# Last output tile in two column halves with a bank and a store each, and q transposes of loop rounds 3 to 5 one place later behind the row transposes

## The chip, the core and the metric

The kernel runs on one core of a Trainium2 chip. The metric is the device time of one execution in microseconds (us); less is better. Before the change the median of four runs is 278.32 us (277.8 to 278.83).

The core has a matrix engine (TensorE, PE in the profile; its weight loads are the row PEld), a vector engine (VectorE, DVE), a scalar engine (ScalarE, ACT), GpSimd (POOL) and SyncE (SP). Each runs its own instructions in order. SP, ACT and POOL can issue DMAs; their issuing sides are SPq, ACTq and POOLq in the profile. Sixteen DMA engines carry all transfers. Matrix products are accumulated in PSUM, which has eight banks.

## What is computed

Attention without softmax, RMS-normalised for each head, and then a two-layer network with a PReLU:

```python
kv  = einsum('bhsd,bhse->bhde', k, v)            # 8 batches, 8 heads, 576 rows, 64 columns
out = einsum('bhsd,bhde->bhse', q, kv)
x   = out / sqrt(mean(out*out, -1) + 1e-6) * g_norm   # reshaped to 4608 tokens x 512
h   = x @ w_in                                   # 512 -> 2048
g   = maximum(h, 0) + alpha * minimum(h, 0)
y   = g @ w_out                                  # 2048 -> 512, float32
```

## The kernel before

**Blocks and rounds.** The 4608 tokens are worked in nine blocks of 512 (`W`, `NW`). After a head part for block 0, a loop `for w in range(1, NW)` (L929) runs rounds of 16 units `u` each. A unit of round `w` issues one group of the first layer for block `w` (`m1_group`, L488: four matmuls of 512 columns at L472, one ACT instruction at L479 and one DVE instruction at L483), seven matmuls of the second layer for block `w - 1` (`prod_mm`, L608, matmul at L631), and the part of the attention for block `w + 1` that a table assigns to that unit (`attention`, L906). All engine orders are written out by hand (a manual schedule): instructions run on each engine in the order in which the code issues them.

**The second layer as seven products.** Tokens, hidden units and output columns are each cut in two, and the product is put together from seven half-size products instead of eight. Each product has 16 matmuls of 256 columns: `i` counts them, `a, c = divmod(i, 8)`, `a` is the group of 128 tokens and `c` the step of the sum. Their order is `Y_ORDER = (1, 6, 2, 7, 5, 4, 3)` (L685). Products 1 and 2 go to PSUM bank X (pool `ps_y`), 6, 7 and 4 to Y (bank `h0`), 5 and 3 to Z (pool `ps_q`). `y_read` (L656) reads partial sums from the banks: the four output quarters are c11, c22, c21 and c12. In the last round (`w == NW - 1`) bank Z is split by `a` (`y_bank`, L592): `yZ0` stays in `ps_q`, `yZ1` takes bank `h2`, which the first layer no longer uses.

**The tail.** After the loop only products are left, for block 8 (L972 to L989). The last 16 matmuls are product 3: eight for `a = 0`, then `y_read(w, "c12", (0,))` adds `yZ0` to a stored partial sum (`u2`) on DVE (L678) and stores 128 rows by 256 columns; then eight for `a = 1`, and the last line, L989, does the same with `yZ1`. That last tile is rows 4224 to 4351, columns 256 to 511, of the output. Product 5 uses the same two Z banks and is read by `y_read(w, "c22")`. The stores take their queue in turn from `store_engines` (`put`, L505; the DMA's line is L508). Output tiles in SBUF come from one pool of four buffers (`ysb_p`, L63), used in rotation.

**Transposes on SP.** From block 4 on (`W_ROW = 3`) the attention output is computed by rows: for each of four row tiles `i` of a block, `rows_mm` (L405, matmuls at L414, L420 and L424), `rows_ssq`, `rows_rs` and `rows_norm` (L449: a DVE instruction at L452 that writes `x_rows`, and then a transposing DMA on SP at L457 that writes 128 columns of `xt`, the input of the next block's first layer). In units 5, 7, 9 and 11 (`norm` in `ATT_ROW`, L894) the row tiles 0 to 3 are normalised and their transposes issued. The q of a later batch is transposed by the same queue: `dma_t` (L333) issues up to five transposing DMAs (L338), one for 128 rows of q each, the fifth for the 64 that remain. When it does so is said by a table:

```python
QT_AT = {False: {7: (0, 1), 9: (2,), 11: (3, 4)}, True: {8: (0,), 10: (1,), 12: (2, 3, 4)}}
...
if w + 1 < B:
    dma_t(w + 1, QT_AT[w == W_ROW].get(u, ()))
```

`attention(w + 1, u)` is called in round `w`, so the `False` row serves the loop rounds 3, 4 and 5, which transpose q of batches 5, 6 and 7. The `True` row serves round 2. In units 7, 9 and 11 a q transpose stands on SP behind the row transpose of the same unit and ahead of the row transpose of the next. GpSimd loads the k, q and v of a later batch at the start of each round (`load_gated`, L186); its first load writes the buffer that the fifth q transpose of the round before has read.

Of the kernel before, what the change touches and what calls it, by code (L numbers as in the profile page):

```python
# [9 lines left out]
FP32 = mybir.dt.float32  # L10
# [7 lines left out]
def kernel(  # L18
# [11 lines left out]
    nc = tc.nc  # L30
# [5 lines left out]
    P = 128  # L36
    NPAIR = H // 2
    W = 512
    NW = N_TOK // W
# [23 lines left out]
    ysb_p = ctx.enter_context(tc.tile_pool(name="ysb", bufs=4))  # L63
    ps_h = ctx.enter_context(tc.tile_pool(name="psh", bufs=1, space=bass.MemoryType.PSUM))
# [12 lines left out]
    def early_pair(eng, nm, tag):  # L77
# [14 lines left out]
            name=nc.get_next_instruction_name(),  # L92
# [25 lines left out]
    for r in range(P // D):  # L118
        nc.sync.dma_start(
            out=alpha_row[NF : NF + 1, r * D : (r + 1) * D], in_=g_norm[:].unsqueeze(0)  # L120
# [7 lines left out]
    for i in range(NBUF):  # L128
        t = {}
        for nm in ("k", "v", "q") if i < 2 else ("k", "v"):  # L130
            n = 1 if nm == "v" else T0 if i == 0 else NT
# [201 lines left out]
    def dma_t(b, ts=tuple(range(NT))):  # L333
        qt = qt_sb[b % 2][:, :, PAD : PAD + S]
        for t in ts:
            c0, c1 = t * P, min((t + 1) * P, S)
            src = stages[b, "q"][:, t] if t < TPP else buf_of(b, "q")[0:REM, TPP]
            nc.sync.dma_start_transpose(  # L338
                out=qt[:, :, c0:c1], in_=src.rearrange("p h d -> p (h d)"),
            )  # L340
        for j in range(NPAIR):
            qts[b, j] = qt_sb[b % 2][:, j, PAD : PAD + S]
# [159 lines left out]
    store_engines = [(nc.gpsimd,)]  # L502
    store_turn = [0]

    def put(dst, src):  # L505
        engs = store_engines[0]
        store_turn[0] += 1
        engs[store_turn[0] % len(engs)].dma_start(out=dst, in_=src)  # L508

    def row_pieces(n0):  # L510
        i = 0
        while i < P:
            b, r = divmod(n0 + i, S)
            np_, nt = (P0, T0) if b == 0 else (P, TPP)
            if b < B_NAT and r < np_ * nt:
                t, p = divmod(r, np_)
                cnt = min(P - i, np_ - p)
                yield i, cnt, b, t, p
            else:
                cnt = P - i if b >= B_NAT else min(P - i, S - r)  # L520
                yield i, cnt, None, n0 + i, 0
            i += cnt

    def grid(b):
        np_, nt = (P0, T0) if b == 0 else (P, TPP)
        return out[b * S : b * S + np_ * nt, :].rearrange("(p t) m -> p t m", t=nt)

    def store_rows(n0, src, c0, c1):
        for i, cnt, b, t, p in row_pieces(n0):
            dst = out[t : t + cnt, c0:c1] if b is None else grid(b)[p : p + cnt, t, c0:c1]  # L530
            put(dst, src[i : i + cnt])
# [7 lines left out]
    HC = D_MODEL // 2  # L539
    NK = NF // 2  # L540
# [48 lines left out]
    ybank = {}  # L589
    part = {}  # L590

    def y_bank(w, n, a):  # L592
        pool, tag = {"X": (ps_y, "y"), "Y": (ps_h, "h0"), "Z": (ps_q, "q")}[n]
        if w == NW - 1 and n == "Z":
            key = (w, n, a)
            if a == 1:
                pool, tag = ps_h, "h2"
            if key not in ybank:
                t = pool.tile([P, HC], FP32, name=f"yZ{a}", tag=tag)
                ybank[key] = t  # L600
                return t[:], True
            return ybank[key][:], False
        fresh = (w, n) not in ybank
        if fresh:
            ybank[w, n] = pool.tile([P, 2, HC], FP32, name=f"y{n}", tag=tag)
        return ybank[w, n][:, a, :], fresh

    def prod_mm(w, n, i):  # L608
        a, c = divmod(i, NK)
        bank, fresh = y_bank(w, {1: "X", 2: "X", 6: "Y", 7: "Y", 4: "Y", 5: "Z", 3: "Z"}[n], a)  # L610
        cols = slice(a * P, (a + 1) * P)
        hi_cols = slice(HW + a * P, HW + (a + 1) * P)
        k, r = divmod(c, 2)
        if n == 1:
            lhs = gts[w, k][:, r, cols]
        elif n == 2:
            lhs = gts[w, k + KQ][:, r, cols]
        elif n == 4:
            lhs = gts[w, k + KQ][:, r, hi_cols]
        else:  # L620
            lhs = sums[w, {6: 2, 7: 3, 5: 1, 3: 4}[n], k][:, r, cols]
        q, rr = divmod(c, GW)
        if n == 1:
            rhs = w_out_sb[q][:, rr, 0:HC]
        elif n == 2:
            rhs = w_out_sb[q + WQ // 2][:, rr, 0:HC]
        elif n == 3:
            rhs = w_out_sb[q + WQ // 2][:, rr, HC:D_MODEL]
        else:
            rhs = wsum[{4: 4, 5: 1, 6: 2, 7: 3}[n]][:, c, :]  # L630
        nc.tensor.matmul(  # L631
            out=bank, lhsT=lhs, rhs=rhs, start=fresh, stop=(c == NK - 1), skip_group_check=True,
        )

    def quad_out(w, r, h, src, subs=(0, 1)):
        n0 = w * W + r * HW
        if n0 >= B_NAT * S and len(subs) == 2:
            put(
                out[n0 : n0 + HW, h * HC : (h + 1) * HC].rearrange("(a p) m -> p a m", p=P),
                src[:],  # L640
            )
            return
        one, two = list(row_pieces(n0)), list(row_pieces(n0 + P))
        if len(subs) == 2 and all(
            x[2] is not None and (*x[:3], x[3] + 1, x[4]) == y for x, y in zip(one, two)
        ):
            for i, cnt, b, t, p in one:
                put(
                    grid(b)[p : p + cnt, t : t + 2, h * HC : (h + 1) * HC],
                    src[i : i + cnt],  # L650
                )
            return
        for a in subs:
            store_rows(n0 + a * P, src[:, a, :], h * HC, (h + 1) * HC)

    def y_read(w, what, subs=(0, 1)):  # L656
        if what == "p1":
            part[w, 1] = u_p.tile([P, 2, HC], FP32, name="p1")
            nc.scalar.copy(out=part[w, 1][:], in_=ybank[w, "X"][:])
            return  # L660
        if what in ("u2", "u3"):
            part[w, what] = u_p.tile([P, 2, HC], FP32, name=what)
            nc.vector.tensor_add(
                out=part[w, what][:], in0=ybank[w, "Y"][:], in1=part[w, 1][:]
            )
            return
        y_sb = ysb_p.tile([P, 2, HC], FP32, name="y_sb")
        if what == "c11":
            nc.scalar.copy(out=y_sb[:], in_=ybank[w, "X"][:])
        else:  # L670
            other = part[w, {"c21": 1, "c22": "u3", "c12": "u2"}[what]]
            if what == "c21":
                nc.vector.tensor_add(out=y_sb[:], in0=ybank[w, "Y"][:], in1=other[:])  # L673
            elif w < NW - 1:
                nc.vector.tensor_add(out=y_sb[:], in0=ybank[w, "Z"][:], in1=other[:])
            else:
                for a in subs:
                    nc.vector.tensor_add(  # L678
                        out=y_sb[:, a, :], in0=ybank[w, "Z", a][:], in1=other[:, a, :]
                    )  # L680
        if w < NW - 1:
            store_engines[0] = (nc.sync if what == "c12" else nc.gpsimd,)
        quad_out(w, int(what[1]) - 1, int(what[2]) - 1, y_sb, subs)

    Y_ORDER = (1, 6, 2, 7, 5, 4, 3)  # L685
    Y_LIST = [(n, i) for n in Y_ORDER for i in range(2 * NK)]
    PER = len(Y_LIST) // NF
# [21 lines left out]
    def h_at(i):  # L709
# [7 lines left out]
        out=alpha_ps[:], lhsT=alpha_row[0 : NF + 1, 0:P], rhs=ident[0 : NF + 1, 0 : NF + 1],  # L717
# [6 lines left out]
        out=beta_sb[:], in0=alpha_ps[:, 0:NF], scalar1=-1.0, scalar2=1.0, op0=ALU.mult, op1=ALU.add,  # L724
# [176 lines left out]
                at_row.setdefault(at if what == "kv" else at + d, []).append((what, j))  # L901
        ATT_ROW[first] = at_row
    ROWS = {"kv": row_kv, "mm": rows_mm, "ssq": rows_ssq, "rs": rows_rs, "norm": rows_norm}
    QT_AT = {False: {7: (0, 1), 9: (2,), 11: (3, 4)}, True: {8: (0,), 10: (1,), 12: (2, 3, 4)}}

    def attention(w, u):  # L906
        if W_ROW <= w < NW:
# [3 lines left out]
            if w + 1 < B:  # L911
                dma_t(w + 1, QT_AT[w == W_ROW].get(u, ()))
        elif w < NW:
# [15 lines left out]
    for w in range(1, NW):  # L929
        if w + 2 < B:  # L930
            load_gated(w + 2)
        for u in range(NF):
            if w >= W_ROW - 1 and u in R_FIRST:
                y_read(w - 1, R_FIRST[u])
# [12 lines left out]
            if w > 2 and u == 0:  # L947
                y_read(w - 2, "c12")
# [23 lines left out]
    w = NW - 1  # L972
    store_engines[0] = (nc.sync, nc.scalar)
    Y_READS[13] = Y_READS.pop(14)
    for u in range(NF):
        unit_sums(NW, u)
        if u == 0:
            y_read(w - 1, "c12")
        for i in range(u * PER, (u + 1) * PER):
            prod_mm(w, *Y_LIST[i])  # L980
            if i == len(Y_LIST) - NK - 1:
                y_read(w, "c12", (0,))
        for what in Y_READS.get(u, ()):
            if what == "c21":
                store_engines[0] = (nc.scalar, nc.gpsimd, nc.sync, nc.gpsimd)
                store_turn[0] = -1
            y_read(w, what)
            store_engines[0] = (nc.sync, nc.scalar)
    y_read(w, "c12", (1,))  # L989


# [28 lines left out]
```

## Time and profile before

| | |
|---|---|
| median of four runs | 278.32 us (277.8 to 278.83) |
| the profiled execution | 278.83 us |
| its span, first to last instruction | 277.1 us |
| outside the span | 1.73 us (278.83 - 277.1) |
| PE busy | 269.3 us, 97% of the span |
| DVE busy | 231.6 us, 84% |
| ACT busy | 155.7 us, 56% |
| last matmul of the chain ends | 273.57 us |
| last DVE addition | 273.65 us, lasts 0.42 us |
| last store issued (SP) | 274.10 us, 128 KB |

A line of the profile's tables gives the line of the kernel, the engine, the operation, the output and the inputs by their names in the program (numbers of buffers left out), the shape, and the count. A timeline or chain line begins with the start in us from the beginning of the span and the duration in us. A duration of a DMA-issuing instruction is the time that its queue took to issue it; the time to landing is counted from there to the arrival of the data and is shown in the table of DMA issues. Matmuls are pipelined, so the time of one in a stream is the distance between starts, not the duration that its own row shows.

### The profile page before, as it was taken

What the parts mean: (1) busy time and instruction counts of PE and PEld (TensorE: products, weight loads), DVE (VectorE), ACT (ScalarE), POOL (GpSimd) and SP (SyncE); (2) the same over time, 40 slices, a digit from 0 to 9 for tenths busy, and PEclk for the clock granted to TensorE, in tenths of its full rate; (3) what the DMA queues carried; (4) which work ended last, traced back from release to release, by engine and by line L of the source; (5) the groups of instructions that cost most, each with busy time, mean ns of one, the idle gap of its engine ahead of it and who ended that gap; (6) DMA issues with size and microseconds to landing.
All of it is one profiled execution on the core that took longest, in us unless ns stands there. A gap on an engine that the chain in (4) does not pass through costs nothing.

```text
span 277.1 us, 5185 instructions
## 1 busy us (share of the span) xinstructions
PE 269.3 (97%) x1928; PEld 173.3 (63%) x1928; DVE 231.6 (84%) x446; ACT 155.7 (56%) x285; POOL 84.4 (30%) x119
## 2 busy tenths in 40 slices
PE   7899999999999999999999999999999999999994
PEld 2434544555766676667666766676666666666784
DVE  7559739988789979997999889988997999887862
ACT  3567447789989846654565456545545554444210
POOL 8743453670913337229121731100111011000200
PEclk9999999999999999999999999999999999999999
DMA  7999999999996579979985799520322032201223
GB/s 152 193 207 198 198 202 189 208 127 177 139 173 109 126 105 140 176 171 121 182 144 117 111 172 174 126 78 0 78 76 78 0 83 73 76 0 40 74 81 114
DMA packets 86621, 34.53 MB, mean 125 GB/s; under 512 B 58804, under 2 KB 84932, under 8 KB 86596
## 3 DMA queue, kind: packets, MB, share of 16 engines
q0 software_dynamic: 57488, 24.35, 67.1%
q1 hardware_dynamic: 28212, 8.90, 16.3%
q10 hardware_dynamic: 896, 0.95, 1.1%
q8 instruction: 15, 0.25, 0.4%
q14 instruction: 10, 0.08, 0.1%
HBM read 36.71 MB, written 9.44 MB: 167 GB/s over the span
## 4 chain that ended last, share of the span: by engine, by line
PE 79%; DMA 12%; DVE 4%; issue 1%; ACT 1%; POOL 1%; DVEq 0%; ACTq 0%; POOLq 0%
PE h_ps L472 37%; PE yY L631 14%; PE yX L631 10%; PE yZ L631 9%; DMA w_in_sb<-in_moe_w_in_dram 5%; DMA vst<-in_v_dram 5%; PE kv_ps L348 3%; DMA qst<-in_q_dram 2%; PE y L497 2%; PE or_ps L414 2%; DVE gt L483 1%; PE ot_ps L370 1%; DVE x_rows L452 1%; PE ssq_ps L386 1%; DVE xt L395 1%
## 5 line engine op out<-in xcount | busy, mean ns | idle before, releaser
L472 PE MATMUL h_ps<-xt,w_in_sb 128*128 128x512 f16 x576 | 145.2, 379 | 0.4 <-DVE y_sb L673 0.2
L479 ACT ACTIVATE m_sb<-h_ps 128x512 f32<-128x512 f32 x144 | 86.1, 599 | 82.0 <-PE h_ps L472 80.4
L483 DVE SCALAR_TENSOR_TENSOR gt<-m_sb,beta_sb,h_ps 128x512 f16<-128x512 f32 x144 | 106.9, 745 | 24.7 <-ACT m_sb L479 21.7
L472 PEld LDWEIGHTS <-w_in_sb 128*128 128x128 f16 x576 | 54.6, 98 | 42.9 <-issue 1.0
L508 POOL DMA_DIRECT2D out_dram<-y_sb x36 | 23.2, 647 | 140.3 <-ACT rstd_r L444 43.8
L631 PEld LDWEIGHTS <-s 128*128 128x128 f16 x512 | 50.1, 98 | 19.2
L631 PEld LDWEIGHTS <-gt 128*128 128x128 f16 x384 | 37.6, 98 | 14.8
L631 PE MATMUL yY<-wsum,s 128*128 128x256 f16 x256 | 36.3, 273 | 0.0
L631 PE MATMUL yX<-w_out_sb,gt 128*128 128x256 f16 x256 | 35.1, 273 | 0.0
L159 POOL DMA_DIRECT2D qst<-in_q_dram x20 | 17.7, 917 | 2.0 <-DMA vst<-in_v_dram 2.0
L631 PE MATMUL yZ<-w_out_sb,s 128*128 128x256 f16 x128 | 17.6, 273 | 0.0
L631 PE MATMUL yZ<-wsum,s 128*128 128x256 f16 x128 | 17.6, 273 | 0.0
L631 PE MATMUL yY<-wsum,gt 128*128 128x256 f16 x128 | 17.6, 273 | 0.0
L429 ACT ACTIVATE sq_sb<-or_ps 128x512 f16<-128x512 f32 x24 | 14.3, 598 | 5.7 <-PE or_ps L414 4.6
L497 PE MATMUL y<-w_out_sb,gt 128*128 128x512 f16 x64 | 16.6, 379 | 0.0
L452 DVE TENSOR_TENSOR x_rows<-or_ps,rstd_r 128x512 f16<-128x512 f32 x24 | 16.4, 684 | 0.0
L435 DVE TENSOR_REDUCE ssq_r<-sq_sb 128x8 f32<-128x512 f16 x24 | 16.3, 680 | 0.0
L583 DVE TENSOR_TENSOR s<-s,gt 128x512 f16<-128x512 f16 x32 | 13.5, 422 | 0.5
L581 DVE TENSOR_TENSOR s<-gt 128x512 f16<-128x512 f16 x32 | 13.4, 419 | 0.0
L587 DVE TENSOR_TENSOR s<-gt,s 128x512 f16<-128x512 f16 x32 | 13.2, 419 | 0.0
L348 PEld LDWEIGHTS <-ksb 128*128 128x128 f16 (+1 forms) x164 | 10.5, 98 | 4.1 <-DMA vst<-in_v_dram 1.1
L356 DVE TENSOR_TENSOR kv_sb<-kv_ps,mask 128x128 f16<-128x128 f32 x32 | 8.1, 285 | 5.7 <-PE kv_ps L348 5.7
(81 smaller groups left out, 251.7 us busy)
## 6 DMA issues: line engine op xcount, KB each, us to landing
out_dram<-y_sb POOLq DMA_DIRECT2D x16, 256.0 KB, 2.7
kst<-in_k_dram POOLq DMA_DIRECT2D x7, 512.0 KB, 7.9
vst<-in_v_dram POOLq DMA_DIRECT2D x7, 512.0 KB, 10.0
qst<-in_q_dram POOLq DMA_DIRECT2D x20, 128.0 KB, 7.5
w_out_sb<-in_moe_w_out_dram POOLq DMA_DIRECT2D x8, 256.0 KB, 12.3
w_in_sb<-in_moe_w_in_dram POOLq DMA_DIRECT2D x3, 512.0 KB, 13.3
out_dram<-y_sb SPq DMA_DIRECT2D x5, 256.0 KB, 2.2
qst<-in_q_dram POOLq DMA_DIRECT2D x2, 512.0 KB, 13.6
```

The lines of the kernel that those rows point to most:

```text
L159: nc.gpsimd.dma_start(out=st[:, t, :, :], in_=srcs["q"][b, :, t * P : (t + 1) * P, :].rearrange("h p d -> p h d"),)
L348: nc.tensor.matmul(out=kv_ps[:], lhsT=ks(t), rhs=vs(t), start=(t == 0), stop=(t == n_runs(b) - 1),)
L429: nc.scalar.activation(out=sq[:], in_=o_ps[:], func=AF.Square)
L435: nc.vector.tensor_reduce(out=ssq[:], in_=sq[:].rearrange("p (h d) -> p h d", h=H), axis=mybir.AxisListType.X, op=ALU.add,)
L452: nc.vector.tensor_tensor(out=xr[:], in0=o_ps[:].rearrange("p (h d) -> p h d", h=H), in1=rstd[:].unsqueeze(2).to_broadcast([P, H, D]), op= ...
L472: nc.tensor.matmul(out=h_ps[:], lhsT=w_in_blk(c, g), rhs=xts[w][:, c, :], start=(c == 0), stop=(c == NC - 1),)
L479: nc.scalar.activation(out=m_sb[:], in_=h_ps[:], func=AF.Relu, scale=-1.0)
L483: nc.vector.scalar_tensor_tensor(out=gts[w, i][:, r, :], in0=m_sb[:], scalar=beta_sb[:, g : g + 1], in1=h_ps[:], op0=ALU.mult, op1=ALU.add,)
L497: nc.tensor.matmul(out=y[:], lhsT=gt_cols(w, g, a * P, (a + 1) * P), rhs=w_out_blk(g), start=(g == 0), stop=(g == NF - 1),)
L508: engs[store_turn[0] % len(engs)].dma_start(out=dst, in_=src)
L583: nc.vector.tensor_sub(out=t[:], in0=sums[w, 1, k][:], in1=a11)
L631: nc.tensor.matmul(out=bank, lhsT=lhs, rhs=rhs, start=fresh, stop=(c == NK - 1), skip_group_check=True,)
```

## The change

Two parts, both in the order that is written out by hand.

1. **The tail.** The Z bank for `a = 1` of the last block becomes two banks: `yZ1` in `h2` for its columns 0 to 127 and the new `yZ2` in `h1` for columns 128 to 255. Every matmul of products 5 and 3 with `a = 1` in the last block becomes two of 128 columns, each with its own weight load. The addition for c22 becomes three DVE instructions in place of two. The last eight matmuls are taken out of the loop: all eight steps of the first column half are issued, then its addition, then its store on ACT; then the second half, its addition, and its store on SP. Each half takes an output buffer of its own.
2. **The table for q.** In rounds 3 to 5 the q transposes are issued as 0 in unit 7, 1 in unit 9, and 2, 3 and 4 in unit 11, in place of 0 and 1, 2, and 3 and 4.

```diff
@@ y_bank
             if key not in ybank:
                 t = pool.tile([P, HC], FP32, name=f"yZ{a}", tag=tag)
                 ybank[key] = t
+                if a == 1:
+                    t = ps_h.tile([P, HC], FP32, name="yZ2", tag="h1")
+                    ybank[w, n, 2] = t
                 return t[:], True
             return ybank[key][:], False
@@ prod_mm
-    def prod_mm(w, n, i):
+    def prod_mm(w, n, i, parts=(0, 1)):
         a, c = divmod(i, NK)
-        bank, fresh = y_bank(w, {1: "X", 2: "X", 6: "Y", 7: "Y", 4: "Y", 5: "Z", 3: "Z"}[n], a)
+        name = {1: "X", 2: "X", 6: "Y", 7: "Y", 4: "Y", 5: "Z", 3: "Z"}[n]
+        bank, fresh = y_bank(w, name, a)
...
+        if w == NW - 1 and name == "Z" and a == 1:
+            for h in parts:
+                half = slice(h * P, (h + 1) * P)
+                nc.tensor.matmul(
+                    out=ybank[w, "Z", 1 + h][:, half], lhsT=lhs, rhs=rhs[:, half],
+                    start=fresh, stop=(c == NK - 1), skip_group_check=True,
+                )
+            return
@@ y_read
-                for a in subs:
-                    nc.vector.tensor_add(
-                        out=y_sb[:, a, :], in0=ybank[w, "Z", a][:], in1=other[:, a, :]
-                    )
+                for a, c in [(0, slice(0, HC))] * (0 in subs) + [(1, slice(0, P)), (1, slice(P, HC))]:
+                    if a in subs:
+                        nc.vector.tensor_add(
+                            out=y_sb[:, a, c], in0=ybank[w, "Z", a + (c.start > 0)][:, c],
+                            in1=other[:, a, c],
+                        )
@@ the table for q
-    QT_AT = {False: {7: (0, 1), 9: (2,), 11: (3, 4)}, True: {8: (0,), 10: (1,), 12: (2, 3, 4)}}
+    QT_AT = {False: {7: (0,), 9: (1,), 11: (2, 3, 4)}, True: {8: (0,), 10: (1,), 12: (2, 3, 4)}}
@@ the last round
-        for i in range(u * PER, (u + 1) * PER):
+        for i in range(u * PER, min((u + 1) * PER, len(Y_LIST) - NK)):
             prod_mm(w, *Y_LIST[i])
...
-    y_read(w, "c12", (1,))
+    for h in range(2):
+        half = slice(h * P, (h + 1) * P)
+        for n, i in Y_LIST[-NK:]:
+            prod_mm(w, n, i, (h,))
+        y_sb = ysb_p.tile([P, 2, HC], FP32, name="y_sb")
+        nc.vector.tensor_add(
+            out=y_sb[:, 1, half], in0=ybank[w, "Z", 1 + h][:, half], in1=part[w, "u2"][:, 1, half]
+        )
+        store_engines[0] = (nc.scalar if h == 0 else nc.sync,)
+        store_rows(w * W + P, y_sb[:, 1, half], HC + h * P, HC + (h + 1) * P)
```

## The prediction

> **What bounds the kernel now.** I read the engine table and the slices first, then what PE waited for, then the tail.
>
> ```profile
> PE 269.3 (97%) x1928; PEld 173.3 (63%) x1928; DVE 231.6 (84%) x446; ACT 155.7 (56%) x285; POOL 84.4 (30%) x119
> PE   7899999999999999999999999999999999999994
> ```
>
> PE is busy in 97% of the span. Its slices are full from the third to the last but one, so idle time lies at the two ends. The busy share alone can hide small gaps, so I asked for PE's waits from 90 us to the end. The columns are total us, times, longest:
>
> ```profile
> PE h_ps L472 <- DVE y_sb L673: 0.2, 1, 0.2
> ```
>
> That is the whole answer: one wait of 0.2 us, on DVE. None is on a transposing DMA. The chain of waits has four 512-column matmuls in 0.86 us and seven 256-column ones in 0.77 us in every unit (109.4 ns for one of 256: 1.75 us for 16). So the middle is the sum of PE's matmuls. Only fewer or cheaper matmuls there, or a shorter tail, can move the time. The tail, from the timeline (start, duration, then the instruction):
>
> ```profile
> 271.54 1.74 PEld L631 LDWEIGHTS <-s 128*128 128x128 f16 x16
> 271.65 1.91 PE L631 MATMUL yZ<-w_out_sb,s 128*128 128x256 f16 x16
> 272.72 0.42 DVE L678 TENSOR_TENSOR y_sb<-yZ,u 128x256 f32<-128x256 f32 x1 [0.18 <-PE yZ L631]
> 273.65 0.42 DVE L678 TENSOR_TENSOR y_sb<-yZ,u 128x256 f32<-128x256 f32 x1 [0.51 <-PE yZ L631]
> ```
>
> and the last two stores in the table of DMA issues (KB each, us to landing):
>
> ```profile
> out_dram<-y_sb ACTq DMA_DIRECT2D x1, 128.0 KB, 1.9
> out_dram<-y_sb SPq DMA_DIRECT2D x1, 128.0 KB, 1.7
> ```
>
> PE ends at 273.57 in the chain, DVE adds from 273.65 to 274.07, SP issues the store at 274.10, it lands 1.7 us later (275.8), and 1.3 us of closing synchronisation fill the span of 277.1. This is one serial path: each term on it counts in full. Before the store lands, the DMA share stands at 0.98 and 1.05 in the half microseconds from 273.5 and 274.0 (stores of c21 and of the tile before), 0.35 in the next and 0.74 from 275.0 to 275.5. So the last store's bytes move alone, after some 0.9 us without them.
>
> **Part 1, the tail, step by step.**
>
> *PE.* Sixteen matmuls of 256 columns (eight of product 5, eight of product 3, `a = 1`) become 32 of 128 with 32 weight loads. Matmuls of 128 columns with a weight load each stand in the trace; in the chain:
>
> ```profile
> 125.39 0.56 PE kv_ps L348 x10
> ```
>
> Ten take 0.56 us, 56 ns each, and the timeline has their starts 0.05 to 0.06 us apart. So 32 x 0.056 - 16 x 0.1094 = 1.79 - 1.75 = **+0.04 us**. Bounds: half of a 256-column one (54.7 ns, +0.00) and the duration of one weight load, 98 ns, if loads did not overlap (32 x 0.098 - 1.75 = +1.39). I take 56, because that row has the same shape, data type and load for every matmul; its bursts are of ten, and the tail's are of 16, which is what stays open.
>
> The Trainium skill, "TensorE: Matmul & The Clock Gate", section "Back-to-back issue gap", speaks against this step: it gives 81 ns for each 128-column matmul in a sustained stream of load and matmul pairs, and about 56 ns only for isolated ones. The row above has 56 inside a stream. By the page's figure PE's term would be 32 x 0.081 - 1.75 = +0.84, an estimate from the page, and the whole change would cost about half a microsecond.
>
> *DVE at the end.* The last addition covers 128 columns in place of 256. Rows of this shape: 128x512 f32 688 ns, 128x256 422 ns, so 133 ns less for each halving step of 128 columns, 289 ns; the 128x128 product at L356 takes 285. Gain 0.42 - 0.29 = **-0.13 us**. The first half's addition needs its eight matmuls (done 0.45 us before PE's end, at 273.16), runs from 273.24 to 273.53 and is gone before the second begins at 273.69. The second waits for the c22 store to release its buffer: that store is issued at 270.56, later by about 0.2 because c22's addition of 0.42 becomes two of 0.29, and lands 2.2 us later, near 273.0. It is clear by 0.7 us; were it late, only this last addition would wait, with nothing else behind it on DVE.
>
> *The stores.* The first half's store stands on ACT behind the store of the tile before (issued 273.2, 0.38 us to issue), so it goes at about 273.6 and lands by 275.3, ahead of the other. The second goes on SP at 274.02 and carries 64 KB in 512-byte pieces in place of 128 KB in 1024-byte ones: 128 pieces as before, eight on each of 16 engines if spread evenly. The page's queue table gives the price of a piece: q1 has 28212 packets, 8.90 MB and 16.3% of 16 engines' span, so 25.6 ns for a mean of 315 bytes; q10 has 896, 0.95 MB and 1.1%, so 54 ns for 1060. On that line 512 bytes cost about 33 ns and 1024 about 53: eight save 8 x 20 ns = **-0.15 us**. Bounds: nothing (a piece costs the same at any size) and -0.21 (half the bytes, half of 8 x 53 ns). The fixed rest of the 1.7 us stays.
>
> *Sum of part 1:* 0.04 - 0.13 - 0.15 = -0.24 us; with the bounds of the stores -0.09 to -0.30.
>
> **Part 2, the q transposes.** It removes and adds no instruction; five transposes for each of three rounds stay on SP. What moves, as the timeline of SP shows it in round 3 (two are merged in the first line):
>
> ```profile
> 113.50 3.18 SPq L338 DMA_TRANSPOSE qt_sb<-qst  x2
> 116.77 1.22 SPq L457 DMA_TRANSPOSE xt<-x_rows  x1
> 118.09 1.22 SPq L338 DMA_TRANSPOSE qt_sb<-qst  x1
> 119.40 1.23 SPq L457 DMA_TRANSPOSE xt<-x_rows  x1
> ```
>
> DVE has the third row tile ready at 115.59 (114.90 + 0.69) and its transpose is issued at 116.77, 1.2 us late; the fourth is ready at 119.02 and issued at 119.40, 0.4 late. Round 4: 0.5 and 0.8 late; round 5: 0.5 and 0.0. After the change one q transpose (1.22 us) fewer stands ahead of each, so these delays mostly go. What they are worth: the last `xt` transpose of round 3 lands at 119.40 + 3.2 = 122.6, and the next round's first matmul on it is at 123.60, after PE has finished other work; in round 5, 175.38 + 2.3 = 177.7 against 180.09. PE never waits for it. Worth **0**; what hides it is PE's own queue of matmuls, with 1.0 to 2.4 us of cover. Were the cover gone, a late tile would cost its delay, at most 1.2 us a round.
>
> What comes later: the last q transpose, by 0.2 to 1.0 us. Behind it on POOL waits the q load of the next round (124.98 in round 4), and behind that k, q and v. The k load goes at 126.37 and lands in 8.2, at 134.6; its first reader is the ACT copy at 142.30. v lands at 131.41 + 10.0 = 141.4 against matmuls at 153.50. The q columns themselves are first read by the row matmuls at 136.55. All have over 7 us of cover. Cost 0; without cover, up to 1.0 us a round.
>
> **Sum:** 278.83 - 0.24 = 278.59 for the profiled execution. That execution is the slowest of the four; taken off the median, 278.32 - 0.24 = **278.08 us**. Four runs spread over 1.0 us; I hold a difference of 0.3% (0.83 us) to be what a measurement of this kernel can tell from none.
>
> **Rivals.**
>
> *The tail does not shorten (278.3).* If a 512-byte piece costs what a 1024-byte one does and the first half's store, on ACT behind another, delays the second's by sharing the engines, -0.09 is all that is left, or +0.1 with that delay. For it: the DMA share is about 1.0 from 273.5 to 274.5. Against it: it has fallen to 0.35 when the last bytes come. 15%.
>
> *The narrow matmuls go at the pace of weight loads (279.4), slower.* Place: the 32 pairs of products 5 and 3. At pace p the change is 32p - 1.75 - 0.28 us: the kernel is slower from p = 63 ns, and by over 0.83 us from p = 89 ns. At 98 ns it is +1.1, 279.4. For it: a weight load lasts 98 ns and at 256 columns stays covered. Against it: the kv burst, where loads overlap at 56 ns. 7%.
>
> *The row transposes did bind in executions that were not profiled (277.3), faster.* Four runs fall in two pairs, 277.8 and 277.92 against 278.72 and 278.83. If transposes landing late make the slow pair, freeing them gives 0.8 more. Against it: the profiled one is of the slow pair and shows no such wait. 7%.
>
> **How the numbers follow.** My forecast, 278.08, has 71%, the first rival 15%, the others 7% each. Within 0.3%: 71 + 15 = 86%; faster 7%, slower 7%. The range takes the term's bounds and the scatter of the runs, about 0.5 us to each side of the median: 277.5 to 278.8.
>
> **What would show it.** Right: last PE matmul at about 273.6, 128-column matmuls 56 ns apart in bursts of 16, last addition 0.29 us, last landing 1.5 to 1.6 us after issue, span 276.9; `xt` transposes issued within 0.2 us of `x_rows`, PE's waits in the middle unchanged. Wrong: starts of matmuls in the tail 80 ns or more apart, a DVE wait for the c22 store, an SP or ACT issue that waits, or a PE wait that appears or goes in rounds 3 to 6.

## The result and the profile after

The changed kernel took 277.88 us (median of 51 runs, 277.11 to 278.84) against 278.32 us (79 runs of the kernel before, 277.53 to 279.37). The ratio is 0.9984, 95% interval 0.9978 to 0.9991: 0.44 us faster, between 0.25 and 0.61. The forecast was 278.08 us, with a range of 277.5 to 278.8 and 86% for "within 0.3%"; all three hold. The last says little, since no change at all would have met it too.

The profiled execution spans 275.92 us, 1.14 us less than the one before (277.06). That is not the size of the change: most of it arises before the tail begins, as the chain of the tail shows (start, duration, what):

```profile
260.40 1.75 PE yX L643 x16
262.15 1.75 PE yY L643 x16
263.89 1.75 PE yX L643 x16
265.64 1.75 PE yY L643 x16
267.39 0.87 PE yZ L643 x8
268.26 0.89 PE yZ L638 x16
269.15 1.75 PE yY L643 x16
270.90 0.87 PE yZ L643 x8
271.77 0.91 PE yZ L638 x16
272.68 0.02 issue
272.70 0.29 DVE y_sb L1008
```

The same chain of before:

```profile
261.33 1.75 PE yX L631 x16
...
271.81 1.76 PE yZ L631 x16
273.57 0.04 DVEq L678
273.61 0.04 issue
273.65 0.42 DVE y_sb L678
```

The first burst shown, `yX`, is the last-but-six burst of 16 matmuls. It begins at 261.33 before and at 260.40 after, 0.93 us apart, at a point where both kernels have issued the same work. So a whole span can't be compared with another. I count from markers inside the trace instead: the **body**, from the first `kv_ps` burst of round 4 to the `yX` burst, and the **tail**, from there to the span's end.

| kernel | span | kv burst | yX burst | body | tail | of it to the last store's issue on SP | from there to the end |
|---|---|---|---|---|---|---|---|
| before | 277.06 | 125.39 | 261.33 | 135.94 | 15.73 | 12.77 | 2.96 |
| after | 275.92 | 124.46 | 260.40 | 135.94 | 15.52 | 12.62 | 2.90 |

The body is the same to 0.01 us. It begins behind the start of round 4, though, where the row transposes of round 3 are first needed, so I take one stretch more, from the first `kv_ps` burst of round 3 to that of round 4: 97.34 to 125.39 before and 96.41 to 124.46 after, 28.05 us in both. The tail is **0.21 us** shorter: 0.15 before the last store is issued and 0.06 after it.

The stores of the tail, in the table of DMA issues of after (KB each, us to landing; the last landing has no time in it):

```profile
out_dram<-y_sb ACTq DMA_DIRECT2D x1, 128.0 KB, 2.0
out_dram<-y_sb ACTq DMA_DIRECT2D x1, 64.0 KB, 1.8
out_dram<-y_sb SPq DMA_DIRECT2D x1, 64.0 KB
```

What PE waited for from 90 us to the end, in after:

```profile
PE h_ps L472 <- DMA xt<-x_rows: 0.2, 1, 0.2
```

One wait of 0.2 us as before, with another releaser. It falls at the start of round 3 (near 94.5 us), ahead of the first table entry that the change moved. SP's timeline of round 3, where before had 116.77 and 119.40 for the two row transposes:

```profile
112.62 2.20 SPq L338 DMA_TRANSPOSE qt_sb<-qst  x1
114.92 1.22 SPq L457 DMA_TRANSPOSE xt<-x_rows  x1
116.23 1.70 SPq L338 DMA_TRANSPOSE qt_sb<-qst  x1
118.12 1.19 SPq L457 DMA_TRANSPOSE xt<-x_rows  x1
119.42 2.58 SPq L338 DMA_TRANSPOSE qt_sb<-qst  x2
```

DVE ends these two `x_rows` at 114.66 and 118.10: the third is issued 0.3 us after that, the fourth at once. Part 2 does what its table says, and in these two profiles nothing waited for a row transpose in rounds 4 to 6.

### The profile page after: what moved, and what is told of

It is laid out like the page before. It is cut to its first block, busy times and chain, and to the rows that moved or that the text cites. A ratio compares the mean times of both kernels' runs of the same rounds, so it can differ in the third digit from the quotient of the medians.

```text
span 275.9 us, 5222 instructions
## 1 busy us (share of the span) xinstructions
PE 269.6 (98%) x1944; PEld 173.6 (63%) x1944; DVE 231.4 (84%) x448; ACT 155.6 (56%) x285; POOL 84.3 (31%) x119
## 3 DMA queue, kind: packets, MB, share of 16 engines
q10 hardware_dynamic: 1040, 1.02, 1.2%
## 4 chain that ended last, share of the span: by engine, by line
PE 84%; DMA 8%; DVE 4%; ACT 1%; issue 1%; DVEq 0%; ACTq 0%; POOLq 0%
PE h_ps L472 40%; PE yY L643 14%; PE yX L643 10%; PE yZ L643 8%; DMA vst<-in_v_dram 7%; PE kv_ps L348 4%; PE y L497 2%; PE or_ps L414 2%; PE ot_ps L370 1%; DVE gt L483 1%; DMA xt<-x_rows 1%; PE ssq_ps L386 1%; DVE xt L395 1%; PE qt_ps L304 1%; PE yZ L638 1%
## 5 line engine op out<-in xcount | busy, mean ns | idle before, releaser
L643 PEld LDWEIGHTS <-s 128*128 128x128 f16 x496 | 48.5, 98 | 19.1
L643 PE MATMUL yZ<-wsum,s 128*128 128x256 f16 x120 | 16.7, 273 | 0.0
L643 PE MATMUL yZ<-w_out_sb,s 128*128 128x256 f16 x120 | 16.7, 273 | 0.0
## 6 DMA issues: line engine op xcount, KB each, us to landing
qst<-in_q_dram POOLq DMA_DIRECT2D x2, 512.0 KB, 13.1
```

Of the source, the lines that this page charges most:

```text
L643: nc.tensor.matmul(out=bank, lhsT=lhs, rhs=rhs, start=fresh, stop=(c == NK - 1), skip_group_check=True,)
```

## The experiments

**Theory:** the tail gives all of the gain, through a shorter last addition and a smaller last store, at almost no cost on PE; the q transposes give nothing, because PE's matmuls cover the row transposes. **Rivals:** the q transposes give some 0.2 us in executions that were not profiled (the measured 0.44 is more than the 0.24 forecast); the gain is not in the store; narrow matmuls pay for their weight loads.

### Each part alone, and a null

One kernel with part 1 alone, one with part 2 alone, the changed kernel again, and the kernel before timed as if it were another. The edit of the two parts, from the kernel before:

```diff
# part 2 alone
-    QT_AT = {False: {7: (0, 1), 9: (2,), 11: (3, 4)}, ...
+    QT_AT = {False: {7: (0,), 9: (1,), 11: (2, 3, 4)}, ...
# part 1 alone: the whole diff without this line
```

> The changed kernel again, on the chip and in the rounds of the three runs beside it. The theory on record (the tail gives -0.24 us, the moved q transposes 0) expects a ratio to the kernel before of 0.9991. The rival, that the q transposes give some 0.2 us of their own, expects 0.9984 as in the result. Both expect in the trace: 16 matmuls of 128 columns at 0.056 us each in the last burst, and the last store issued 12.6 us after the last-but-six burst of 16 begins.

> The tail alone: two banks, two additions and two stores for the last tile; the table for q as before. The theory on record expects the whole gain here: ratio 0.9991 (-0.24 us), and the same as the run with both parts. The rival (q transposes worth about 0.2 us) expects 0.9991 here too, but the run with both parts lower by 0.0007.

> The table for q alone; the tail as before. The theory on record expects ratio 1.0000, PE without any wait on a row transpose in rounds 3 to 6, and the third and fourth row transposes issued within 0.2 us of their x_rows. The rival expects 0.9993 (-0.2 us), or more, with waits that the profile of before does not show.

> The kernel before, unchanged, timed as if it were another one: every theory expects 1.0000. How far the ratio lies from it, and how wide its interval is, says what the three runs beside it can tell: 0.24 us is 0.0009.

| kernel | ratio to before | 95% interval | body | tail |
|---|---|---|---|---|
| both | 0.9988 | 0.9977 to 0.9999 | 135.94 | 15.54 |
| part 1 alone | 0.9992 | 0.9978 to 1.0007 | 135.94 | 15.51 |
| part 2 alone | 0.9998 | 0.9985 to 1.0011 | 135.95 | 15.73 |
| before, as a null | 1.0005 | 0.9989 to 1.0021 | 135.94 | 15.73 |

The times alone settle little: the null itself lies 0.0005 off, and each interval is wider than the effect. The markers settle it for the profiled executions. Body and tail repeat to 0.03 us, while the place of the `yX` burst runs from 259.78 (the null) to 261.33 (before), in two executions of the same program. Part 1 has the whole 0.2 us of the tail; part 2 has nothing in body or tail.

The stretch ahead of the body is another matter. From the first `kv_ps` burst of round 3 to that of round 4 it is 28.04 to 28.06 us in ten of the 13 profiles other than the one with q at 9 (below), but 28.42 in a later profile of the changed kernel (taken beside the kernel with c21 in halves, below), 28.34 in part 1 alone and 28.23 in the kernel with the cut store. The first of the three, from its chain:

```profile
119.21 3.81 DMA xt<-x_rows
123.02 0.14 issue
123.16 1.02 PE h_ps L472 x4
```

Its last row transpose of round 3 lands at 123.02, and round 4's first matmul, which needs it, starts 0.14 us later and 0.37 late. In the other two that matmul starts 0.13 to 0.14 us after the same transpose has landed (122.57 and 122.60), 0.29 and 0.18 late. The table of PE's waits lists the first alone, with 0.2 us. So row transposes do bind in some executions: in two of four profiles with the table of before, and in one of eight with that of part 2. These counts are too small to say whether part 2 makes it rarer, and the timing of part 2 alone, from 0.42 us faster to 0.31 slower, can't say it either.

### More of part 2, and its opposite

All five q transposes behind the last row transpose (unit 11), and all five ahead of it (unit 9):

```diff
-    QT_AT = {False: {7: (0, 1), 9: (2,), 11: (3, 4)}, ...
+    QT_AT = {False: {11: (0, 1, 2, 3, 4)}, ...      # late
+    QT_AT = {False: {9: (0, 1, 2, 3, 4)}, ...       # at 9
```

> The kernel before with all five q transposes in unit 11, behind the last row transpose, in rounds 3 to 5: more of part 2 than the change does. If row transposes that stand behind q ones cost anything, this gains more than part 2 alone; the theory on record expects 1.0000, a stretch of 135.94 us from the first kv burst of round 4 to the last-but-six burst, and the q load of the next round up to 2 us later without anything waiting for it.

> The kernel before with all five q transposes in unit 9, ahead of the last row transpose, in rounds 3 to 5. The theory that PE's queue of matmuls covers the row transposes by 1.0 to 2.4 us, and no more, expects the last row transpose 4 us later in each round and PE to wait 2 to 3 us for it at the start of rounds 4, 5 and 6, some 7 us in all (285 us). If row transposes have far more cover than that, 278.3 us and no wait.

Late: ratio 1.0000 (0.9983 to 1.0016), body 135.94, tail 15.72, and 28.05 for the stretch ahead of the body. With every q transpose out of the way nothing is gained in the profile; its interval is too wide to exclude some 0.1 us. The loads behind the last q transpose on POOL came 3.5 us later in round 4 in place of the expected 2, and nothing waited for them.

At 9: 291.73 us in one run, beside 278.66 for the kernel before in one. What PE waited for from 90 us on, and the first of the three waits in the chain:

```profile
PE h_ps L472 <- DMA xt<-x_rows: 10.3, 3, 3.8
```

```profile
121.82 0.42 ACT m_sb L479
122.24 3.72 DMA xt<-x_rows
125.96 0.05 issue
126.01 1.41 PE h_ps L472 x4
```

The direction and the place are as expected, the size is not: 13.1 us in place of 7. By the markers, from the first `kv_ps` burst of round 3 to the `yX` burst (178.11 us against 163.99), it is 14.1 us. The waits are 3.5, 3.8 and 3.0 us; the last row transpose, issued at 122.24, takes 3.7 us to land here (2.3 to 3.2 in before). And after the first two waits PE is slow: four matmuls of 512 columns take 1.41 us where they took 0.86. The stretches behind the first wait and, in the last line, behind the third (PE, PEld, DVE, ACT and POOL busy with counts, granted PE clock, DMA share, GB/s):

```profile
126.00:128.00 2.00, 1.99 (x8) 1.06 (x9) 0.00 (x0) 0.55 (x1) 2.00 (x4) 0.63 1.11 71
128.00:130.00 2.00, 2.00 (x16) 1.67 (x15) 1.88 (x4) 0.05 (x1) 2.00 (x3) 0.51 1.31 157
130.00:132.00 2.00, 2.00 (x21) 1.49 (x20) 0.73 (x2) 0.60 (x1) 1.21 (x2) 1.00 1.99 167
194.00:196.00 2.00, 2.00 (x22) 1.46 (x21) 1.48 (x3) 0.49 (x1) 0.00 (x0) 1.00 0.03 8
```

These are means over 2 us. In stretches of half a microsecond the clock is 1.00 until 126.5, then 0.50 to 0.55 until 130.0, and 1.00 again: half speed for 3.4 us. The second wait is followed by the same, the third, of 3.0 us, by full clock. Two stretches of 3.4 us at half speed cost PE 2 x 1.7 = 3.4 us, which is nearly all of the remaining 14.1 - 10.3 = 3.8. The order on SP matters once the cover that the prediction read off is gone.

### Where in the tail the gain is

Two kernels that each have one piece of part 1, run and profiled once each. One keeps the two banks, narrow matmuls and two additions, but stores the tile at once; the other keeps one bank and one addition and only cuts the store.

```diff
# one store (from the changed kernel)
+    y_sb = ysb_p.tile([P, 2, HC], FP32, name="y_sb")
     for h in range(2):
...
-        y_sb = ysb_p.tile([P, 2, HC], FP32, name="y_sb")
...
-        store_engines[0] = (nc.scalar if h == 0 else nc.sync,)
-        store_rows(w * W + P, y_sb[:, 1, half], HC + h * P, HC + (h + 1) * P)
+    store_engines[0] = (nc.sync,)
+    store_rows(w * W + P, y_sb[:, 1, :], HC, D_MODEL)
# cut store (from the kernel before)
-    y_read(w, "c12", (1,))
+    y_sb = ysb_p.tile([P, 2, HC], FP32, name="y_sb")
+    nc.vector.tensor_add(out=y_sb[:, 1, :], in0=ybank[w, "Z", 1][:], in1=part[w, "u2"][:, 1, :])
+    for h in range(2):
+        store_engines[0] = (nc.scalar if h == 0 else nc.sync,)
+        store_rows(w * W + P, y_sb[:, 1, h * P : (h + 1) * P], HC + h * P, HC + (h + 1) * P)
```

> The changed kernel with its two banks, 32 narrow matmuls and two additions, but one output buffer and one 128 KB store on SP for the last tile. Measured in the trace from the start of the last-but-six burst of 16 matmuls to the span's end (15.73 us before, 15.52 with the whole change). The theory on record, -0.09 us from PE and DVE and the rest from the 64 KB store, expects 15.64. If all of the gain were in the shorter addition, 15.53.

> The kernel before with one thing changed: its last addition of 128x256 is stored by two DMAs of 128 columns, on ACT and SP at the same time, from one bank and one addition. If it is enough that the last DMA carries half the bytes, the stretch from the last-but-six burst to the span's end falls from 15.73 to about 15.6. If what counts is that half of the bytes were sent before, it stays at 15.73 or grows, since both halves still move at the end.

| kernel | tail | to the last store's issue on SP | from there to the end |
|---|---|---|---|
| before | 15.73 | 12.77 | 2.96 |
| one store | 15.60 | 12.62 | 2.98 |
| cut store | 15.90 | 12.78 | 3.12 |
| after | 15.52 | 12.62 | 2.90 |

The narrower last addition with its matmuls is worth 0.15 us up to the issue; the smaller store, in the changed kernel, 0.06 to 0.08 more. The cut store alone costs 0.17: two 64 KB stores sent at the same moment end later than one of 128 KB. Here a smaller last store paid only where the other half had left before. Why it pays so little is in the DMA shares. In the cut store the 512-byte pieces move alone, and in before 1024-byte ones fill the engines (share and GB/s are the last two columns):

```profile
274.16:274.46 0.30, 0.00 (x0) 0.00 (x0) 0.00 (x0) 0.00 (x0) 0.00 (x0) 1.00 0.99 297
```

```profile
273.96:274.26 0.30, 0.00 (x0) 0.00 (x0) 0.12 (x1) 0.00 (x0) 0.00 (x0) 1.00 1.04 348
```

By these, with 16 engines, a piece of 512 bytes takes 512 x 16 x 0.99 / 297 = 27 ns and one of 1024 takes 49. Eight pieces for each engine should have saved 0.18 us; 0.06 were seen. In after the engines are still full when the last store's bytes come, from 273.92 on:

```profile
273.50:274.00 0.50, 0.00 (x0) 0.00 (x0) 0.00 (x0) 0.00 (x0) 0.00 (x0) 1.00 1.03 308
274.00:274.50 0.50, 0.00 (x0) 0.00 (x0) 0.00 (x0) 0.00 (x0) 0.00 (x0) 1.00 0.41 118
```

From 273.92 to 274.40 the table of DMA queues counts 46 packets on ACT's queue (q10), which carries the other stores here. In before there are none behind the last store's first packet.

### Taking the backlog away

If the last bytes share the engines because those of c21 and of the other c12 tile have pushed the first half back, sending c21 sooner must give the rest of the 0.18 us back. So c21 is added and stored in two halves by rows, the first on SP, and the other tile of c12 goes to SP too:

```diff
+            if what == "c21" and w == NW - 1:
+                for a in range(2):
+                    nc.vector.tensor_add(
+                        out=y_sb[:, a, :], in0=ybank[w, "Y"][:, a, :], in1=other[:, a, :]
+                    )
+                    store_engines[0] = (nc.sync if a == 0 else nc.scalar,)
+                    store_rows(w * W + HW + a * P, y_sb[:, a, :], 0, HC)
+                return
...
             if i == len(Y_LIST) - NK - 1:
+                store_engines[0] = (nc.sync,)
                 y_read(w, "c12", (0,))
```

> The changed kernel, and beside it the c21 tile of the last block added and stored in two halves by rows (SP, then ACT) and the tile before the last stored on SP, so that 128 KB of c21 leave 0.3 us sooner. If the last store's data wait behind the c21 and c12 bytes on the DMA engines, the stretch from the last-but-six burst to the span's end falls from 15.52 to 15.4. If only the fixed part of the last DMA counts, it stays at 15.52.

> The kernel with c21 stored in two halves by rows, now timed. Its trace gave a stretch from the last-but-six burst to the end of 15.39 us, 0.34 less than before: expected ratio 0.9988, and 0.0005 below the changed kernel beside it. If traces of single executions misled, the same as the changed kernel.

> The changed kernel beside the two. By its traces 0.21 us less than before: ratio 0.9992. The rival that the moved q transposes give some 0.2 us more in executions without a profile expects 0.9985 or less.

Tail 15.39 in both of its profiles: 12.62 to the issue of the last store, as in the changed kernel, and **2.77** from there to the end (274.01 to 276.78 in the first). Against 2.96 before, that is 0.19 us, where the piece price asks for 0.18. The records of single packets in the traces show the place: the last store's last bytes move 1.36 us after its issue in before, 1.28 in after and 1.20 here (1.19 in the second profile), and the other stores' last bytes 0.66, 1.07 and 0.84 after it, while its own first ones come at 0.83 to 0.89. So 0.16 of the 0.19 lie in the data, and the backlog was what the changed kernel lost. (ACT, with one store less ahead of it, also issues the first half 0.08 us sooner; the two effects were not taken apart.) Timed, the ratio is 0.9973 (0.9959 to 0.9987), 277.50 us, beside 0.9988 (0.9974 to 1.0001), 277.80 us, for the changed kernel. The first has the lowest ratio of this study, beyond its interval against the kernel before; against the changed kernel the order is that of the traces, but the intervals overlap.

### An uneven cut

The last tile cut at column 192 in place of 128, on top of the kernel with c21 in halves. The same cut stands in the additions and the store:

```diff
-                half = slice(h * P, (h + 1) * P)
+                half = slice(0, P + 64) if h == 0 else slice(P + 64, HC)
```

> The same with the last tile cut at column 192 of 256 in place of 128, so that the last eight matmuls, the last addition and the last store are of 64 columns. If a weight load and a matmul of 64 columns go in 28 ns, as half of 56, the matmuls cost nothing (8 x (0.082 + 0.028) = 0.88 us a burst), the addition falls by 0.07 and the stretch to 15.2 to 15.3 us. If a floor of 56 ns for each weight load binds, each of the two bursts grows by 0.22 us and the stretch is 15.7 us.

Ratio 0.9985 (0.9974 to 0.9996), body 135.94, tail 15.64, 0.25 more than with the even cut. The matmuls are not to blame. Its chain:

```profile
268.07 0.89 PE yZ L638 x16
...
271.59 0.68 PE yZ L638 x8
272.26 0.03 DVEq L1017
```

Sixteen narrow matmuls of product 5 take 0.89 us as in the even cut. In product 3 eight of 192 columns take 0.68, and eight of 64 follow, whose starts in the trace are 29 ns apart (272.08 to 272.29), every one with a weight load of its own. So no floor of 56 ns for each weight load shows. What the cut lost is elsewhere. The last store is issued 12.65 us after the `yX` burst, 0.03 later than with the even cut, and from there (272.86) to the end it is 2.99 us in place of 2.77, although that store has only 32 KB. The chain ends on DVE's own last instruction and names no store, but the packets do. The first part's store, 96 KB in pieces of 768 bytes, was issued on ACT at 272.73, only 0.13 us sooner, and its bytes move until 274.06. The last store's bytes come from 273.87 to 274.18, the first of them 1.02 us after the issue in place of 0.83, the last 1.33 in place of 1.20. So the two stores share the engines again, and 32 KB end later than 64 KB did. The expectation had no term for the first part's bytes. Some 0.09 us between the last bytes and the end stay without a cause.

## Why the prediction was right, point by point

**What bounds the kernel.** Right: the body is 135.94 or 135.95 us in 13 of the 14 profiles of this study; only the kernel with q at 9, whose row transposes were delayed past their cover, differs (145.32). At the start of round 4, ahead of the body, it is PE's matmuls in ten of these 13 and a row transpose in three.

**PE, +0.04 us.** Right: the bursts of 16 narrow matmuls take 0.89 and 0.91 us where eight wide ones take 0.87, and from the `yX` burst to PE's end it is 12.28 us against 12.24. The 81 ns that the Trainium skill, "TensorE: Matmul & The Clock Gate", section "Back-to-back issue gap", gives for each 128-column matmul in a sustained stream is not what this chip showed: 0.91 / 16 = 57 ns in a burst where each matmul has its own weight load. The measurement decides; the rival that rested on weight loads is dead.

**DVE, -0.13 us.** Right in size (0.42 to 0.29), and a little short as a term: from the `yX` burst to the last issue 0.15 were gained where 0.04 - 0.13 = -0.09 were forecast. The other 0.06 lie between PE's last matmul and the addition, 0.08 us before and 0.02 after. Ends of matmuls are modelled in the profile, so whether that is a real wait stays open.

**The stores, -0.15 us.** The mechanism is right and the size is not: -0.06. (The prediction's 8 x 20 ns is 0.16; its 0.15 is rounded down.) The piece price was nearly right (20 ns saved for each piece by the queue table, 22 by the stretches). The first half's store did land ahead of the other. What failed is the reading of before, "the last store's bytes move alone", carried over to after. In before the other stores' bytes have moved 0.2 us before the last store's first; in after the first half, held up by c21 and the other c12 tile, moves until 274.10, while the last store's bytes come from 273.92. That is the first rival in a mild form, sharing of the engines; the kernel with c21 in halves showed it by taking it away. The sign "last landing 1.5 to 1.6 us after issue" did not come either: the trace's semaphore records have it at 1.75 in after and 1.74 in before. The bytes end 0.08 us sooner, the landing does not, and the 0.06 are gained between landing and end; why is open.

**The sum of part 1.** -0.21 in the trace against -0.24: the two misses nearly cancel. That part of the agreement is luck.

**Part 2, 0.** Right in the profile from which it was read, but not for every execution. "PE never waits for it" rests on a cover of 1.0 us seen once, in round 3. Over 13 profiles the last row transpose of that round landed between 24.2 and 26.7 us after the round's first `kv_ps` matmul, a scatter of 2.5 us, while PE's first matmul on it starts at 26.4 where it does not wait. So the third rival, that row transposes bind in executions that were not profiled, is right in kind and wrong in size: 0.18 to 0.37 us in three of 13 profiles, in place of 0.8. One of the three is of the changed kernel, so part 2 does not end it. Whether part 2 is worth 0 or some 0.1 us is not shown. All q transposes behind gained nothing in one profile, and all in front lost 13 us.

**What stays open.** The median moved by 0.44 us, with 0.25 as the near end of its interval, while the tail gives 0.21. In four later timings too (0.9988 twice for the changed kernel, 0.9973 with c21 in halves, 0.9985 with the uneven cut) the time moved further than the trace by 0.1 to 0.4 us; part 1 alone (0.9992) moved as the trace does. Nothing in body or tail has the rest. The waits at the start of round 4 may have some of it: their mean is 0.12 us over four profiles with the table of before and 0.05 over eight with that of part 2, so as an estimate 0.07 us more, and 0.28 in all, which lies in the interval. So few profiles can't carry that. The changed kernel's 0.9988 beside the kernel with c21 in halves lies between the 0.9992 of the tail alone and the 0.9985 of the rival and settles nothing. What else differs from profile to profile lies before round 3's first `kv_ps` burst, which begins between 95.79 and 97.53 us. That scatter is larger than what is sought. Many profiles of one kernel, which were not taken, could tell whether it is chance.

## What to carry to other kernels

Once one engine is busy throughout, look for gains on the serial path behind its last instruction, and compare traces from markers inside, since whole spans scattered by 1.5 us here for an effect of 0.2. Cutting the last tile paid here where the first part's bytes had left the DMA engines before the second's came; where other bytes still filled them, part of the gain went back. An order of a queue that is covered is worth nothing until the cover is gone, and then all of the wait counts, with more on top. Read such a cover from several executions: one showed 1.0 us here, and the landings it had to cover scattered by 2.5. And see that the markers enclose every place where the change can act.

## What the runs showed of the hardware

- Matmuls with a weight load each ran at 57 ns for 128 columns in bursts of 16 and started 29 ns apart for 64, although each weight load's own row lasts 98 ns.
- After waits of PE of 3.5 and 3.8 us its granted clock was 0.5 for 3.4 us, and 128-column matmuls took twice as long (ten in 1.07 us in place of 0.56); after a wait of 3.0 us it stayed at 1.0. The Trainium skill, "TensorE: Matmul & The Clock Gate", section "What's actually happening", describes a gate that opens only after a window of activity of about 3.4 us; the 3.4 us of these rows agree.
- Stores in pieces of 512 bytes moved at 297 GB/s with the engines full, those of 1024 at 348. Two half stores sent at once ended 0.16 us later than the whole one.
